# Threshold attention and Fourier mixing: the softmax sums closed by one reduce, and two small jobs moved from GpSimd to ScalarE

## The chip, the cores and the metric

The kernel runs on one core of a Trainium2 chip. The metric is the device time of one execution in microseconds (us); lower is better. Five engines work side by side, each through its own queue in program order: TensorE (PE; its weight loads are listed as PEld), VectorE (DVE), ScalarE (ACT), GpSimd (POOL), and SyncE (SP), which here issues nearly all DMAs.

## The reference

Attention with a threshold, followed by a Fourier mixing block with a two-layer network. B = 8 batches, 8 heads, 576 rows, head dimension 64, so a model width of 512; all in float32 (the two weight matrices arrive in float64 bits).

```python
scores = scale * np.matmul(q, k.transpose(0, 1, 3, 2))
thresh = np.max(scores, axis=-1, keepdims=True) - tau
scores = np.where(scores >= thresh, scores, -1000000000.0)
scores = scores - np.max(scores, axis=-1, keepdims=True)
attn = np.exp(scores)
attn = attn / (np.sum(attn, axis=-1, keepdims=True) + 1e-09)
x = np.matmul(attn, v)                      # then heads side by side: (B, S, 512)

mixed = np.real(np.fft.fft(np.fft.fft(x, axis=1), axis=2))
u = x + mixed
un = (u - np.mean(u)) / np.sqrt(var + 1e-06)   # mean and var over the last axis
out = u + np.maximum(un @ w_ch1, 0.0) @ w_ch2
```

## The kernel before

The order of all instructions is written out by hand; no planner moves them. The attention is cut into steps. A pair of heads has five steps (`t = i % NT`): in `t` 0 to 3, 128 query rows of both heads, and in `t` 4 the last 64 rows of both heads in one tile of 128 rows, so that such a step has one head column only (`nh` is 1). A batch has four pairs, so 20 steps.

Each step begins with `scores`, on TensorE (L427, L433), into PSUM. The softmax then takes these instructions: the row maximum, negated, on VectorE (L451); exp on ScalarE (L459), and right behind the first exp a small ScalarE instruction that makes the threshold `thr` (L463); then on VectorE the masking (L467), which multiplies the exps by the comparison with the threshold and adds up the row into `den` with an accumulator output. 1e-9 is added to each sum (L472, one element per row, after each head), and both are inverted (L481). The two masked tiles are turned by TensorE in the next step (`transposed_weights(i - 1)`, L578 to L600) and multiplied by v in `weighted_values` (L627).

The inverse sums are used in two ways. In the first two batches (steps 0 to 39) GpSimd copies them with repetition into `rec`, 128 columns (L493); TensorE transposes `rec` beside the last columns of the weights (L581), and the product with v is multiplied by it on VectorE (L636). From step 40 on the weights themselves are scaled, by ScalarE (L540).

q is multiplied by the scale in place before it is transposed: for the first pair and from the third batch on by ScalarE (L385), for the other pairs of the first two batches by GpSimd (L387), in step `t == 2`; VectorE transposes k and q in step `t == 3` (L398 to L401), and only then SyncE loads the next pair into the same tiles.

Three loops run over the steps. `step(i)` for batch 0 adds the conversion of the first weight matrix from float64 bits, in stages over VectorE (L293, L296, L308), ScalarE (L301, L304, L315) and GpSimd (L313, L316), with small TensorE fillers (L111) and the subtraction of column means (L373). `second_batch(i)` for steps 20 to 39 adds the conversion of the second weight matrix, the mixing of batch 0 (L750 to L796), and the first group of the network (`channels`: L877 on TensorE, evacuated alternately by ScalarE, L882, and VectorE, L884). Its filling work is given out by `fill`, from a budget that depends on counts alone and not on time. From step 40 on the third loop uses `softmax_first`, `softmax_second` and `softmax_third`; there the sums of a step get their 1e-9 in one instruction of up to two elements (L531) and are inverted (L534), and the network runs as two levels of a fast matrix product (L1163, L1306 on TensorE, with additions on VectorE and GpSimd).

In `step`, ScalarE's queue holds per step: exp, `thr`, exp, the last conversion stage of the chunk before (L315), the copies of the transposed weights of step i - 1 (L584, L598), and the first stages of the present chunk (L301, L304). In a step with `t == 4`, a copy of 64 weight columns (L497) stands right behind the softmax.

Of the kernel before, what the change touches and what calls it, by code (L numbers as in the profile page):

```python
# [9 lines left out]
FP32 = mybir.dt.float32  # L10
INT32 = mybir.dt.int32
UINT32 = mybir.dt.uint32
ALU = mybir.AluOpType
# [34 lines left out]
def kernel(  # L48
# [12 lines left out]
    nc = tc.nc  # L61
# [5 lines left out]
    NT = 5  # L67
# [305 lines left out]
        eng.tensor_tensor(out=w1[c][:, cols], in0=rows, in1=means[g][:, :], op=ALU.subtract)  # L373


    heads = {}
    steps = {}
    xs = {}
# [2 lines left out]
    def scale_q(n):  # L381

        raw = loaded[n][0]
        if n == 0 or late:
            nc.scalar.activation(out=raw[:, :], in_=raw[:, :], func=ACT.Copy, scale=q_scale[:, :])  # L385
        else:
            nc.gpsimd.tensor_scalar(  # L387
                out=raw[:, :], in0=raw[:, :], scalar1=q_scale[:, :], scalar2=None, op0=ALU.mult
            )

    def prep_pair(n):

# [46 lines left out]
    def softmax(i, between=None, meanwhile=None, behind=None):  # L439


        t = i % NT
        sc, nh = steps[i]
        neg = sb.tile([128, 2], FP32, tag="neg", bufs=3, name="neg")
        thr = sb.tile([128, 2], FP32, tag="thr", bufs=3, name="thr")
        den = sb.tile([128, 2], FP32, tag="den", bufs=3, name="den")


        e = sb.tile([128, 2 * S], FP32, tag="e", name="e")
        for j in range(nh):  # L450
            nc.vector.tensor_reduce(  # L451
                out=neg[:, j : j + 1], in_=sc[j][:, :, 0:HALF], axis=AXIS_XY, op=ALU.max,
                negate=True,
            )
        if meanwhile is not None:
            meanwhile()
        for j in range(nh):
            ej = e[:, S * j : S * (j + 1)].rearrange("p (c n) -> p c n", c=2)
            nc.scalar.activation(  # L459
                out=ej, in_=sc[j][:, :, 0:HALF], func=ACT.Exp, bias=neg[:, j : j + 1], scale=1.0  # L460
            )
            if j == 0:
                nc.scalar.activation(  # L463
                    out=thr[:, 0:nh], in_=neg[:, 0:nh], func=ACT.Identity,
                    bias=thr_off[:, :], scale=-1.0,
                )
            nc.vector.scalar_tensor_tensor(  # L467
                out=ej, in0=sc[j][:, :, 0:HALF], scalar=thr[:, j : j + 1], in1=ej,
                op0=ALU.is_ge, op1=ALU.mult, accum_out=den[:, j : j + 1],
            )  # L470

            nc.vector.tensor_scalar(  # L472
                out=den[:, j : j + 1], in0=den[:, j : j + 1], scalar1=1e-9, scalar2=None,
                op0=ALU.add,
            )
# [5 lines left out]
        nc.vector.reciprocal(den[:, 0:nh], den[:, 0:nh])  # L481
        rec = None
        if normalized(i // NT):
            nc.vector.tensor_scalar(
                out=e[:, 0:S], in0=e[:, 0:S], scalar1=den[:, 0:1], scalar2=None, op0=ALU.mult
            )
            if nh == 2:
                nc.scalar.activation(
                    out=e[:, S : 2 * S], in_=e[:, S : 2 * S], func=ACT.Copy, scale=den[:, 1:2]
                )  # L490
        else:
            rec = sb.tile([128, 2 * D], FP32, tag="rec", name="rec")
            nc.gpsimd.tensor_copy(  # L493
                rec[:, :].rearrange("p (j d) -> p j d", j=nh), _repeated(den[:, 0:nh], 2 * D // nh)
            )
        if t == 4:
            nc.scalar.copy(e[:, S : S + 64], e[:, 512:S])  # L497
        steps[i] = (e, rec)

    def softmax_first(i):  # L500
# [20 lines left out]

    def softmax_second(i):
        sc, nh, e, thr = steps[i]
        den = sb.tile([128, 2], FP32, tag="den", bufs=3, name="den")
        for j in range(nh):
            ej = e[:, S * j : S * (j + 1)].rearrange("p (c n) -> p c n", c=2)
            nc.vector.scalar_tensor_tensor(  # L527
                out=ej, in0=sc[j][:, :, 0:HALF], scalar=thr[:, j : j + 1], in1=ej,
                op0=ALU.is_ge, op1=ALU.mult, accum_out=den[:, j : j + 1],
            )  # L530
        nc.vector.tensor_scalar(  # L531
            out=den[:, 0:nh], in0=den[:, 0:nh], scalar1=1e-9, scalar2=None, op0=ALU.add
        )
        nc.vector.reciprocal(den[:, 0:nh], den[:, 0:nh])  # L534
        steps[i] = (nh, e, den)

    def softmax_third(i):
        nh, e, den = steps[i]
# [878 lines left out]
    def step(i):  # L1417

        n, t = divmod(i, NT)
        scores(i)  # L1420

        def stages(count):
            for _ in range(count if i - 1 in chunks else 0):
                next(chunks[i - 1], None)

        def next_stages():
            stages(2)

        def last_stage():
            stages(1)  # L1430
            chunks.pop(i - 1, None)

        if t == 1 and n > 0:
            softmax(i, lambda: weighted_values(n - 1, 1), next_stages, last_stage)
            load_v(n + 1)
        elif t == 3:
            softmax(i, lambda: weighted_values(n, 0), next_stages, last_stage)
        else:
            softmax(i, None, next_stages, last_stage)
        if t == 1 and n > 0:  # L1440
            pass
        elif later and later[0][0] <= i:
            later.pop(0)[1](i)
        else:
            busy(2 if i < NCHUNK else 1)
        if t == 2:
            scale_q(n + 1)
        if t == 3:
            prep_pair(n + 1)
        if t == 1:  # L1450
            prep_ends(n)
        if i in chunks:
            next(chunks[i])
        if i > 0:
            transposed_weights(i - 1)
        if i in chunks:
            next(chunks[i])
        while after and after[0][0] <= i:
            after.pop(0)[1]()
        if i > 0 and i + 3 < NCHUNK:  # L1460
            chunks[i + 3] = w1_chunk(i + 3)
        if t == 2 and n > 0:
            folds.append(fold_rows(n - 1))
        if folds and next(folds[0], True):
            folds.pop(0)

    folds = []
    later = []
# [91 lines left out]
    def second_batch(i):  # L1560

        nonlocal budget
        n, t = divmod(i, NT)
        first = i - per_batch
        if first != 1:
            scores(i)
        if first == 0:

            transposed_weights(i - 1)
        softmax(  # L1570
            i, None, lambda: (advance(first - 1), advance(first - 1)), lambda: advance(first - 1)
        )
        chunks.pop(first - 1, None)
        transfers(first)
        fold_more()
        if first == 0:
            weighted_values(n - 1, 1)
            scores(i + 1)
            column_means(LAST)
            copy_mean(LAST)  # L1580
            folds.append(fold_rows(n - 1))
            while folds:
                fold_more()
            load_v(n + 1)
            start_batch(0)
            mix(3)
            mix(3)
        elif first == 1:
            mix(3)
            transposed_weights(i - 1)  # L1590
            mix(2)
            mirrored(LAST)
            for c, eng in ((1, nc.vector), (3, nc.vector), (0, nc.gpsimd), (2, nc.gpsimd)):
                less_mean(eng, LAST, c)
            advance(first)
            advance(first)
        elif first == 2:
            mix(2)
            transposed_weights(i - 1)
            mix(2)  # L1600
            weighted_values(n, 0)
            advance(first)
            advance(first)
        else:
            fill()
            transposed_weights(i - 1)
            advance(first)
            advance(first)
# [135 lines left out]
```

## Time and profile before

The median of three runs is 1607.57 us (1606.21 to 1608.24). The profiled execution took 1605.7 us, of which the profile's span is 1603.8 us.

| part | value |
|---|---|
| span, instructions | 1603.8 us, 27061 |
| busy PE | 1537.4 us (96%) |
| busy VectorE | 1105.6 us (69%) |
| busy ScalarE | 908.4 us (57%) |
| busy GpSimd | 811.7 us (51%) |
| L472, add 1e-9, early | 72 instructions, mean 153 ns |
| L531, add 1e-9, late | 120 instructions: 96 of two elements, mean 352 ns; 24 of one, mean 154 ns |
| L493, rec, GpSimd | 40 instructions, mean 387 ns |
| L387, q scaled, GpSimd | 8 instructions, mean 1854 ns |
| L385, q scaled, ScalarE | 24 instructions, mean 771 ns |
| L497, copy of 64 columns, ScalarE | 8 instructions, mean 244 ns |

The page names an instruction group by its line, engine and operation, and by what it writes and reads (`out<-in`). In the order of time a row gives the start and the length in us; a bracket at its end says how long the engine was idle before and what released it. A busy TensorE isn't TensorE at its peak, because matmuls are pipelined and their ends are modelled.

### The profile page before, as it was taken

How to read it: one execution, taken by the hardware profiler on the slowest of the kernel's cores; microseconds unless marked ns; L12 is line 12 of the kernel's file. 1: busy time of each engine (PE TensorE's matmuls, PEld its weight loads, DVE VectorE, ACT ScalarE, POOL GpSimd, SP SyncE). 2: the span in 40 equal slices, each digit the busy share in tenths (PEclk: the TensorE clock that was granted, in tenths of full speed). 3: DMA queues.
4: the chain of work that ended last, by engine and by line, in shares of the span. 5: the costliest groups of instructions: out<-in, count | busy, mean ns of one | idle time of the engine just before them, and what ended most of it. 6: DMA issues, size and time to landing. Idle time of an engine off the chain costs nothing.

```text
span 1603.8 us, 27061 instructions
## 1 busy us (share of the span) xinstructions
PE 1537.4 (96%) x9770; PEld 1189.2 (74%) x9770; DVE 1105.6 (69%) x2165; ACT 908.4 (57%) x1873; POOL 811.7 (51%) x1014
## 2 busy tenths in 40 slices
PE   8999979999999999999999999999999999999997
PEld 4555445555787778877787878787887778879997
DVE  7997886845869566766577566856676656746547
ACT  5774665554655666656666666656665665223121
POOL 6784664034455552536254724455263625537646
PEclk9999999999999999999999999999999999999998
DMA  6423221555956264634564355626463534546655
GB/s 158 131 57 115 75 76 36 175 158 164 291 159 203 72 182 125 182 104 141 141 175 140 113 159 145 191 69 180 123 185 108 154 113 158 191 157 237 235 193 190
DMA packets 245499, 239.05 MB, mean 149 GB/s; under 512 B 196947, under 2 KB 214869, under 8 KB 225014
## 3 DMA queue, kind: packets, MB, share of 16 engines
q1 hardware_dynamic: 242854, 237.02, 49.1%
q8 instruction: 78, 1.28, 0.3%
q10 hardware_dynamic: 2512, 0.30, 0.2%
q14 instruction: 55, 0.45, 0.1%
HBM read 207.50 MB, written 29.62 MB: 148 GB/s over the span
## 4 chain that ended last, share of the span: by engine, by line
PE 76%; DVE 14%; ACT 4%; issue 2%; POOL 2%; DMA 1%; SPq 0%; DVEq 0%; ACTq 0%; POOLq 0%
PE ph L1163 24%; PE po L1306 17%; PE pv L627 8%; PE sc L427 7%; PE pw L596 6%; PE po L901 4%; PE ph L877 2%; PE py L750 2%; DVE e L467 2%; PE sc L433 1%; PE pa L767 1%; PE pe L578 1%; PE pa L771 1%; DVE neg L451 1%; ACT e L512 1%
## 5 line engine op out<-in xcount | busy, mean ns | idle before, releaser
L512 ACT ACTIVATE e<-sc,neg 128x576 f32<-128x576 f32 x216 | 158.6, 734 | 139.8 <-DVE neg L506 139.4
L506 DVE TENSOR_REDUCE neg<-sc 128x1 f32<-128x576 f32 x216 | 154.0, 749 | 112.0 <-PE sc L427 104.1
L1306 PE MATMUL po<-w,w_all 128*128 128x128 f32 x1792 | 229.1, 278 | 0.7 <-ACT ends L584 0.7
L1306 PEld LDWEIGHTS po<-w,w_all 128*128 128x128 f32 x1792 | 214.7, 193 | 10.2 <-issue 5.5
L1100 DVE TENSOR_TENSOR hs<-ph,hs 128x512 f32<-128x512 f32 (+1 forms) x128 | 105.1, 821 | 158.5 <-PE ph L1163 104.0
L1109 POOL TENSOR_TENSOR w<-hs 128x512 f32<-128x512 f32 x32 | 42.1, 1320 | 318.9 <-ACT hs L1105 245.1
L596 PE MATMUL pw<-ident,e 128*128 128x128 f32 x1152 | 172.1, 276 | 18.0 <-ACT x_first L634 9.1
L1163 PE MATMUL ph<-u_t,w 128*128 128x256 f32 x768 | 180.5, 381 | 0.5 <-DMA w<-f 0.4
L527 DVE SCALAR_TENSOR_TENSOR e<-sc,thr,e 128x576 f32<-128x576 f32 x216 | 168.1, 811 | 17.7 <-ACT thr L516 17.7
L427 PE MATMUL sc<-kT,qT 64*128 64x288 f32 x1024 | 170.3, 432 | 7.9 <-DVE e L467 7.9
L598 ACT COPY e_t<-pw 128x512 f32<-128x512 f32 x256 | 148.5, 594 | 45.8 <-PE pw L596 44.6
L540 ACT ACTIVATE e<-e,den 128x576 f32<-128x576 f32 x216 | 157.6, 775 | 16.6 <-DVE den L534 15.4
L596 PEld LDWEIGHTS pw<-ident,e 128*128 128x128 f32 x1152 | 136.3, 142 | 36.3 <-ACT x_first L634 10.1
L1163 PE MATMUL ph<-w_all,w 128*128 128x256 f32 x672 | 157.0, 382 | 2.9 <-DVE hs L1100 1.8
L1163 PEld LDWEIGHTS ph<-u_t,w 128*128 128x128 f32 x768 | 141.2, 190 | 23.4 <-issue 4.4
L1105 ACT ACTIVATE hs<-hs 128x512 f32<-128x512 f32 (+1 forms) x96 | 74.1, 772 | 122.0 <-DVE hs L1100 120.8
L1163 PEld LDWEIGHTS ph<-w_all,w 128*128 128x128 f32 x672 | 123.5, 190 | 25.6 <-issue 6.2
L427 PEld LDWEIGHTS sc<-kT,qT 64*128 64x128 f32 x1024 | 93.9, 186 | 62.9 <-issue 32.8
L1213 POOL TENSOR_TENSOR w_all<-w_all 128x128 f32<-128x128 f32 (+2 forms) x160 | 118.5, 758 | 29.9 <-DVE w_all L1326 22.4
L1306 PE MATMUL po<-w,hs 128*128 128x128 f32 x960 | 126.3, 279 | 0.0
L1306 PEld LDWEIGHTS po<-w,hs 128*128 128x128 f32 x960 | 116.2, 193 | 9.4 <-issue 7.2
L792 POOL TENSOR_TENSOR u_t<-x,tmp 128x289 f32<-128x289 f32 (+1 forms) x45 | 34.5, 766 | 104.8 <-DVE tmp L787 104.8
(221 smaller groups left out, 2985.1 us busy)
## 6 DMA issues: line engine op xcount, KB each, us to landing
w<-f SPq DMA_DIRECT2D x152, 1024.0 KB, 4.9
hs<-in_moe_w_ch_dram SPq DMA_DIRECT2D x23, 512.0 KB, 4.6
q_in<-in_q_dram SPq DMA_DIRECT2D x128, 72.0 KB, 3.9
out_dram<-u SPq DMA_DIRECT2D x36, 256.0 KB, 2.5
k_in<-in_k_dram SPq DMA_DIRECT2D x124, 72.0 KB, 3.0
v_in<-in_v_dram SPq DMA_DIRECT2D x64, 128.0 KB, 4.7
f<-w SPq DMA_DIRECT2D x14, 512.0 KB, 4.0
f<-w SPq DMA_DIRECT2D x7, 1024.0 KB, 4.4
```

Source lines behind the costliest of these rows:

```text
L427: nc.tensor.matmul(sc[j][:, c, 0:HALF], qT[hp, 128 * t : 128 * t + 128], kT[hp, k0 + HALF * c : k0 + HALF * (c + 1)], start=True, stop=True,)
L506: nc.vector.tensor_reduce(out=neg[:, j : j + 1], in_=sc[j][:, :, 0:HALF], axis=AXIS_XY, op=ALU.max, negate=True,)
L512: nc.scalar.activation(out=ej, in_=sc[j][:, :, 0:HALF], func=ACT.Exp, bias=neg[:, j : j + 1], scale=1.0)
L527: nc.vector.scalar_tensor_tensor(out=ej, in0=sc[j][:, :, 0:HALF], scalar=thr[:, j : j + 1], in1=ej, op0=ALU.is_ge, op1=ALU.mult, accum_out ...
L540: nc.scalar.activation(out=e[:, S * j : S * (j + 1)], in_=e[:, S * j : S * (j + 1)], func=ACT.Copy, scale=den[:, j : j + 1],)
L596: nc.tensor.transpose(pw[:, c, :], e[:, c0 : c0 + 128], ident[:, :])
L598: nc.scalar.copy(e_t[:, 4 * j : 4 * j + 4, qs], pw[:, :, :])
L627: nc.tensor.matmul(pv[64 * j : 64 * j + 64, 0:m], vt[:, 2 * c + j, :], e_t[:, 4 * j + c, 0:m] if c < 4 else ends[:, 0, 0:m], start=(c == 0 ...
L1100: nc.vector.tensor_tensor(out=to, in0=bank, in1=to if other is None else other, op=ALU.add)
L1163: nc.tensor.matmul(bank[:, 256 * q : 256 * q + 256].rearrange("p (two n) -> p two n", two=2), left[:, 256 * c + 128 * q : 256 * c + 128 * ...
L1213: return lambda: eng.tensor_tensor(out=to, in0=to, in1=other, op=ALU.add)
L1306: nc.tensor.matmul(to, lefts[m][j][:, s], right_[:, 128 * s : 128 * (s + 1)], start=(jn in (0, 4) or cut and jn > 4) and s == 0, stop=s == ...
```

## The change

Three things are changed.

The 1e-9 is no longer added by an instruction of its own. Three tiles `den_eps` of two columns per head are filled with 1e-9 once. The masking writes each row sum into the first column of its head, so that sum and 1e-9 lie side by side; a reduce over the last axis then gives sum plus 1e-9 for both heads at once, and the reciprocal follows. A helper, `inverse`, does this for all three loops. In the early softmax this also takes the instruction between the two heads' maskings away.

`rec` is written by ScalarE and no longer by GpSimd, by a new function `spread_inverse` that is called at the very end of each step of the first two batches. The copy of 64 columns of `t == 4` moves there too.

q is scaled by ScalarE in all pairs.

```diff
+    den_eps = [const.tile([128, 2, 2], FP32, name=f"den_eps{u}") for u in range(3)]
+    for den in den_eps:
+        nc.vector.memset(den[:, :, :], 1e-9)
+
+    def inverse(i, nh):
+        den = sb.tile([128, 2], FP32, tag="den", bufs=3, name="den")
+        nc.vector.tensor_reduce(
+            out=den[:, 0:nh], in_=den_eps[i % 3][:, 0:nh, :], axis=AXIS_X, op=ALU.add
+        )
+        nc.vector.reciprocal(den[:, 0:nh], den[:, 0:nh])
+        return den
...
     def scale_q(n):
 
         raw = loaded[n][0]
-        if n == 0 or late:
-            nc.scalar.activation(out=raw[:, :], in_=raw[:, :], func=ACT.Copy, scale=q_scale[:, :])
-        else:
-            nc.gpsimd.tensor_scalar(
-                out=raw[:, :], in0=raw[:, :], scalar1=q_scale[:, :], scalar2=None, op0=ALU.mult
-            )
+        nc.scalar.activation(out=raw[:, :], in_=raw[:, :], func=ACT.Copy, scale=q_scale[:, :])
...
             nc.vector.scalar_tensor_tensor(
                 out=ej, in0=sc[j][:, :, 0:HALF], scalar=thr[:, j : j + 1], in1=ej,
-                op0=ALU.is_ge, op1=ALU.mult, accum_out=den[:, j : j + 1],
-            )
-
-            nc.vector.tensor_scalar(
-                out=den[:, j : j + 1], in0=den[:, j : j + 1], scalar1=1e-9, scalar2=None,
-                op0=ALU.add,
+                op0=ALU.is_ge, op1=ALU.mult, accum_out=den_eps[i % 3][:, j, 0:1],
             )
...
-        nc.vector.reciprocal(den[:, 0:nh], den[:, 0:nh])
-        rec = None
+        den = inverse(i, nh)
...
+            steps[i] = (e, None)
         else:
-            rec = sb.tile([128, 2 * D], FP32, tag="rec", name="rec")
-            nc.gpsimd.tensor_copy(
-                rec[:, :].rearrange("p (j d) -> p j d", j=nh), _repeated(den[:, 0:nh], 2 * D // nh)
-            )
-        if t == 4:
+            steps[i] = (e, den[:, 0:nh])
+
+    def spread_inverse(i):
+        e, den = steps[i]
+        if i % NT == 4:
             nc.scalar.copy(e[:, S : S + 64], e[:, 512:S])
+        if den is None:
+            return
+        nh = den.shape[1]
+        rec = sb.tile([128, 2 * D], FP32, tag="rec", name="rec")
+        nc.scalar.copy(
+            rec[:, :].rearrange("p (j d) -> p j d", j=nh), _repeated(den, 2 * D // nh)
+        )
         steps[i] = (e, rec)
...
     def softmax_second(i):
...
-        nc.vector.tensor_scalar(
-            out=den[:, 0:nh], in0=den[:, 0:nh], scalar1=1e-9, scalar2=None, op0=ALU.add
-        )
-        nc.vector.reciprocal(den[:, 0:nh], den[:, 0:nh])
-        steps[i] = (nh, e, den)
+                op0=ALU.is_ge, op1=ALU.mult, accum_out=den_eps[i % 3][:, j, 0:1],
+            )
+        steps[i] = (nh, e, inverse(i, nh))
...
@@ -1463,6 +1464,7 @@   (end of step)
             folds.append(fold_rows(n - 1))
         if folds and next(folds[0], True):
             folds.pop(0)
+        spread_inverse(i)
...
@@ -1624,6 +1626,7 @@   (end of second_batch)
         if first < 3:
             budget += 3 * per_slot
+        spread_inverse(i)
```

More of the change, by code (lines that the diff above doesn't have):

```diff
@@ L445, in softmax @@
         thr = sb.tile([128, 2], FP32, tag="thr", bufs=3, name="thr")
-        den = sb.tile([128, 2], FP32, tag="den", bufs=3, name="den")
         e = sb.tile([128, 2 * S], FP32, tag="e", name="e")
@@ L523, in softmax_second @@
         sc, nh, e, thr = steps[i]
-        den = sb.tile([128, 2], FP32, tag="den", bufs=3, name="den")
         for j in range(nh):
@@ L528, in softmax_second @@
                 out=ej, in0=sc[j][:, :, 0:HALF], scalar=thr[:, j : j + 1], in1=ej,
-                op0=ALU.is_ge, op1=ALU.mult, accum_out=den[:, j : j + 1],
+                op0=ALU.is_ge, op1=ALU.mult, accum_out=den_eps[i % 3][:, j, 0:1],
             )
-        nc.vector.tensor_scalar(
-            out=den[:, 0:nh], in0=den[:, 0:nh], scalar1=1e-9, scalar2=None, op0=ALU.add
-        )
-        nc.vector.reciprocal(den[:, 0:nh], den[:, 0:nh])
-        steps[i] = (nh, e, den)
+        steps[i] = (nh, e, inverse(i, nh))
     def softmax_third(i):
```

## The prediction

> **What bounds the kernel now.** I read the chain of work that ended last, then the busy time by stretch, then the order of time on each engine at the lines that the change touches. The page's chain by engine:
>
> ```profile
> PE 76%; DVE 14%; ACT 4%; issue 2%; POOL 2%; DMA 1%; SPq 0%; DVEq 0%; ACTq 0%; POOLq 0%
> ```
>
> The stretches say where the part that is not TensorE lies (columns: stretch, length, then busy time of PE, PEld, DVE, ACT, POOL, the granted clock, DMA share, GB/s):
>
> ```profile
> 40.00:80.00 40.00, 37.53 (x195) 21.31 (x194) 38.38 (x84) 31.80 (x63) 30.79 (x37) 1.00 0.49 132
> 80.00:120.00 40.00, 36.52 (x184) 20.68 (x184) 37.20 (x81) 28.12 (x57) 32.60 (x37) 0.96 0.25 57
> 400.00:800.00 400.00, 390.94 (x2604) 318.50 (x2604) 279.27 (x542) 251.67 (x514) 191.81 (x241) 0.99 0.55 161
> ```
>
> Up to some 127 us (batch 0, 20 steps) VectorE is full, 37 to 38 of 40 us; TensorE's figure there contains its filler matmuls. From 290 us TensorE is full: 98%, and VectorE at 70% has air. Between 127 and 290 us (batch 1) the chain changes hands. So a microsecond of VectorE is worth most in batch 0 and almost nothing after 290 us.
>
> Inside a step of batch 0, in order of time (start, length, engine, line), first the early softmax, then a late one and its neighbours:
>
> ```profile
> 103.41 0.82 DVE L467 SCALAR_TENSOR_TENSOR e<-sc,thr,e 128x576 f32<-128x576 f32 x1 [0.16 <-ACT thr L463]
> 104.15 0.08 DVE L467 DVE_READ_ACCUMULATOR e<-sc,thr,e 128x1 f32 x1
> 104.27 0.15 DVE L472 TENSOR_SCALAR den<-den 128x1 f32<-128x1 f32 x1
> 104.34 0.81 DVE L467 SCALAR_TENSOR_TENSOR e<-sc,thr,e 128x576 f32<-128x576 f32 x1
> ...
> 105.19 0.15 DVE L472 TENSOR_SCALAR den<-den 128x1 f32<-128x1 f32 x1
> 105.38 0.17 DVE L481 RECIPROCAL den<-den 128x2 f32<-128x2 f32 x1
> ...
> 858.14 0.80 DVE L527 SCALAR_TENSOR_TENSOR e<-sc,thr,e 128x576 f32<-128x576 f32 x1
> 858.88 0.81 DVE L527 SCALAR_TENSOR_TENSOR e<-sc,thr,e 128x576 f32<-128x576 f32 x1
> 859.61 1.27 POOL L1121 TENSOR_TENSOR hs<-hs,w 128x512 f32<-128x512 f32 x1
> 859.73 1.17 DVE L531 TENSOR_SCALAR den<-den 128x2 f32<-128x2 f32 x1
> 860.93 0.17 DVE L534 RECIPROCAL den<-den 128x2 f32<-128x2 f32 x1
> 861.01 0.47 DVE L863 SCALAR_TENSOR_TENSOR u<-w_all,rstd,u 128x256 f32<-128x256 f32 x1
> ```
>
> With the addition of 1e-9 between the heads the second masking starts 0.93 us after the first (104.34 - 103.41); without it, late, 0.74 us. And the late addition, on two elements, took 1.17 us, ending with GpSimd's instruction.
>
> [...] the one-element addition (L472) takes 153 to 155 ns always, the two-element one (L531) has a mean of 352 and a most of 1417 ns. No small reduce is in the trace. [...]
>
> **The change part by part.** Price of the new reduce: L506 reduces 576 elements in 748 ns; [...] against the addition's 153. I take them as equal, an issue distance of 0.19 us (105.38 - 105.19). Bounds: 0.05 less, or 0.10 more if two rows of two cost extra.
>
> *Early additions.* Of 72, 32 go without successor (the first head's in two-head steps) and 40 become reduces. Each of the 32 is worth 0.93 - 0.74 = 0.19 us of VectorE.
>
> *Inverse sums (rec).* 40 GpSimd copies, mean 387 ns, become ScalarE copies. Price: the exp's neighbour L497 copies 64 columns in 244 ns; [...] It stands last in the step. Queued behind it: the next step's exp, thr, hence VectorE's masking; and TensorE waits for rec with its transpose (L581). In batch 0 the queue has no gap just there:
>
> ```profile
> 82.22 0.70 ACT L304 ACTIVATE hs<-hs,shift 128x512 int32<-128x512 int32 x1
> 82.83 0.72 ACT L459 ACTIVATE e<-sc,neg 128x576 f32<-128x576 f32 x1
> ```
>
> I went through the 20 hand-overs from step to step, comparing thr's end with the end of VectorE's instruction before the masking. Seven (steps 1, 8, 12, 15 to 18 to their next) have idle ScalarE or wait for scores: full gain, 7 x 0.19 = 1.33 us. Six are tight, VectorE later than ScalarE by only 0.07 to 0.17: they keep 0.06 to 0.14 each, 0.70 together. Three are set by ScalarE (3, 10, 13): -0.19 + 0.20, nothing. In the four one-head steps (4, 9, 14, 19) nothing is saved, and the copy L497 (244 ns, 0.15 of queue) moves to the step's end too, 0.35 with rec; minus the slack of 0.15 in two of them: 0.22 + 0.21 + 0.36 + 0.35 = 1.14 lost. At 17.88 us TensorE waits 1.92 us for rec, but VectorE only follows at 22.97: 0.3 gained. [...] (0.51 against 0.41 us): 0.1 in about five steps that VectorE sets, 0.5. Batch 0: -1.33 - 0.70 - 0.30 - 0.50 + 1.14 = -1.7 us.
>
> *q scaled (8 copies).* GpSimd 1.85 us each become ScalarE 0.76 (L385), 0.64 of queue. No DMA moves: q's load follows VectorE's transpose. In batch 0 (steps 2, 7, 12, 17) ScalarE waits there 1.33, 0.69, 0.60+0.26 and 1.7 us: covered; without that cover 0.64 each. In batch 1 it stands just before rec; at step 22 the 0.84 us delay falls into VectorE's 1.47 us wait for TensorE (168.79), save 0.1; at 27, 32, 37 ScalarE waits over 3 us.
>
> *Batch 1.* Mix start, step 20: +0.2 (exp behind rec). GpSimd's u_t chain at 156.58 loses a rec: -0.3. Step 22: +0.1. Step 24: copies behind L882, so TensorE's transposes at 175.28 go only at about 177.3; much of it is under VectorE's and ScalarE's chain: +0.4. Steps 25, 27 and 38, masking and reduce: -0.19, -0.3, -0.19; step 28: -0.24. Step 26: ScalarE delivers at 193.9 what GpSimd did at 193.8: 0. Step 29: +0.37; step 31: +0.2; step 34: +0.05. Step 36 is the dearest:
>
> ```profile
> 270.78 0.27 PE L581 MATMUL pe<-ident,rec 128*128 128x128 f32 x1
> ...
> 271.43 0.20 ACT L855 ACTIVATE warm<-eps 128x1 f32<-128x1 f32 x1
> ```
>
> Here rec falls behind two table loads that end with L855, so the transpose comes at about 271.9 in the middle of a TensorE chain: +0.95. The sum is +1.0.
>
> *Late steps.* 120 additions become reduces: [...] nearly all under TensorE. What TensorE does lose there is four stalls like this one (the addition above, 8 us of full VectorE, exp, the copy that frees a bank):
>
> ```profile
> 869.33 0.44 PE L596 MATMUL pw<-ident,e 128*128 128x128 f32 x2 [2.19 <-ACT x_first L634]
> ```
>
> But L863, next on VectorE, [...] 860.88 instead of 861.01. I take 4 x 0.13 = 0.5 us; the bounds are 0 and 4 x 1.0.
>
> Sum: -1.7 + 1.0 - 0.5 = -1.2 us. The profiled execution took 1605.7 (span 1603.8 and 1.9 around it), so 1604.5; the runs' median of 1607.57 lies 1.9 higher, so 1606.4 on its scale.
>
> **Rivals.** [...] If L863 doesn't wait, the four stalls give 4.0 instead of 0.5: 1606.4 - 3.5 = 1602.9. For it: L863's median is 0.48 and many of its neighbours are GpSimd's; against: the tiny two-input L690 took 1.12 us beside GpSimd.
> *ScalarE's queue comes to set the end (slower).* The spread, last in the queue, may be late for TensorE. If rec takes its full 0.30 us because it waits on VectorE's semaphore (20 tight steps, +2.0), and TensorE's waits at steps 24, 29, 31 and 36 count in full (2.05 + 0.45 + 0.70 + 0.95 = 4.15 against my 1.97, +2.2), and the scaling at step 22 isn't covered (+0.6): 1606.4 + 4.8 = 1611.2. It decides once ScalarE ends a step later than TensorE ends the next scores, about 1.2 us. For it: ScalarE was only 0.07 to 0.17 us ahead in six steps. Against: after 227 us ScalarE waits 1 to 4 us per step for its maxima.
> *The reduce is dearer (no change).* 0.10 us x about 25 on the chain: 1608.9. The kernel would still be within the bound. That it isn't executed as written is unlikely; all 160 steps call it.
>
> **Chances and range.** 0.2% is 3.2 us, about what a measurement of this kernel can tell from none. The forecast and the dearer reduce, both within it: 0.48. [...]: 0.27. ScalarE sets the end: 0.25. The likeliest case alone spans 1604.6 to 1609.0; to leave out no more than 2 in 10 the range reaches both rivals, 1601.9 to 1611.4.
>
> **What would show it.** Right: maskings 0.74 us apart in the first 40 steps; reduces of about 0.15 us without a long tail; rec on ScalarE near 0.3 us; a transpose of rec waiting near 271 us; four late stalls still near 2 us, with L863 at 1.2 to 1.3 us in its place; start of the late steps about 0.7 us earlier than 288. Wrong: TensorE waits on ScalarE's rec of over 4 us in all, or the late stalls down to 1.2 us.

## Result: no measurable difference, from two effects of several microseconds

| | before | after |
|---|---|---|
| median | 1607.54 us | 1606.47 us |
| ratio, 95% interval | | 0.9994 (0.9986 to 1.0002) |
| profiled execution, its span | 1605.7, 1603.8 us | 1604.92, 1603.1 us |
| busy VectorE, ScalarE, GpSimd | 1105.6, 908.4, 811.7 us | 1090.0, 919.8, 787.2 us |

The forecast was 1606.4 us. That it came out so near is partly luck, as the experiments show. The moves cost much more than the terms given to them, the reduce gains at least what its terms said but in other places, and the two cancel. Besides, the runs of the changed kernel had a slightly higher clock than those of before (0.9878 against 0.9866), which by the line fitted below is worth about 1 us.

The profile after: the chain by engine, the line that answers to the one of before.

```profile
PE 74%; DVE 15%; ACT 4%; issue 2%; DMA 2%; POOL 2%; SPq 1%; ACTq 0%; DVEq 0%; POOLq 0%
```

The stretches after (stretch, length, then busy time of PE, PEld, DVE, ACT, POOL, the granted clock, DMA share, GB/s):

```profile
40.00:80.00 40.00, 37.20 (x195) 21.00 (x193) 38.11 (x77) 32.88 (x72) 26.39 (x29) 1.00 0.46 127
80.00:120.00 40.00, 35.64 (x175) 20.65 (x176) 36.84 (x75) 29.92 (x65) 31.15 (x35) 0.91 0.25 57
400.00:800.00 400.00, 391.42 (x2599) 319.82 (x2598) 272.89 (x541) 250.84 (x513) 192.59 (x241) 0.99 0.53 160
```

In the first stretch VectorE runs seven instructions fewer (77 for 84), and yet it is as full as before: 38.11 us against 38.38. What the instructions left free, it spends in longer ones. That is the first sign that the saving did not reach the end of the batch. The second stretch has a granted clock of 0.91 (0.96 before), to which the section on the hardware comes back.

The new instructions, each by its line (count, then shortest, median and longest in ns):

```profile
L382 DVE TENSOR_REDUCE den<-den_eps x160: 154/157/158, 15.0 to 1351.9; 128x2 f32<-128x4 f32 x128, 128x1 f32<-128x2 f32 x32
L501 ACT COPY rec<-den x40: 279/286/323, 17.0 to 290.6; 128x128 f32<-128x128 f32 x40
L396 ACT ACTIVATE q_in<-q_in,q_scale x32: 758/762/812, 7.0 to 1297.3; 128x576 f32<-128x576 f32 x32
```

All three prices hold: 157 ns for the reduce (taken as equal to the addition's 153), 286 for rec (near 0.3 us), 762 for the scaling (760). The longest of 160 reduces is 158 ns, beside a GpSimd that is busy half of the time (787.2 of 1603.1 us): none shows a wait like that of the two-element addition, whose longest took 1417 ns. That rec takes 0.20 us of ScalarE's queue was the author's estimate; in this trace the next instruction, where it waits for nothing, starts 186 to 200 ns after rec.

Where the difference of 0.7 us between the two spans comes from can be read at VectorE's reciprocals, of which there is one in each step. Step 20's is at 133.22 us (before 132.89), step 40's at 294.67 (292.30). So the changed kernel enters the late steps 2.4 us later, not 0.7 earlier as predicted, and gains 3.1 us afterwards. Part of each figure goes with the clock. At 104.4 us the changed kernel has a fall of the clock to half that is twice as long (6.8 us) as the one of before at 106.7 (3.4 us); e9 (below), which has the same code there and a single fall, is 0.8 us less behind from step 15 to 17. And 2.65 of the 3.1 us are gained behind the last softmax, where before has such a double fall at 1383 us and the changed kernel none.

The late stall after the change, the same place as the one at 859.73 us before, in the order of time:

```profile
862.65 1.27 POOL L1122 TENSOR_TENSOR hs<-hs,w 128x512 f32<-128x512 f32 x1
862.78 0.16 DVE L382 TENSOR_REDUCE den<-den_eps 128x2 f32<-128x4 f32 x1
862.97 0.17 DVE L385 RECIPROCAL den<-den 128x2 f32<-128x2 f32 x1
863.05 1.15 DVE L864 SCALAR_TENSOR_TENSOR u<-w_all,rstd,u 128x256 f32<-128x256 f32 x1
...
869.57 0.30 PE L579 MATMUL pe<-ident,e 128*128 128x128 f32 x1 [0.25 <-DVE w_all L1327]
872.06 0.79 PE L597 MATMUL pw<-ident,e 128*128 128x128 f32 x4 [2.19 <-ACT x_first L635]
```

The wait for GpSimd has moved from the addition to L864 (L863 before), 0.47 to 1.15 us, which ends 0.28 us behind GpSimd's L1122, and the stall of 2.19 us is still there: both as predicted. The gain sits in the line between: TensorE's wait for `w_all` fell to 0.25 us, from 0.56 in the row of before:

```profile
866.84 0.30 PE L578 MATMUL pe<-ident,e 128*128 128x128 f32 x1 [0.56 <-DVE w_all L1326]
```

The same 0.31 us is gained at four places (at the first, 0.90 became 0.59), 1.25 us in all; the sum had 0.13 each.

### The profile page after: what moved, and what is told of

Read it like the earlier page. It is cut to its first block, busy times and chain, and to the rows that moved or that the text cites. A ratio compares the mean times of both kernels' runs of the same rounds, so it can differ in the third digit from the quotient of the medians.

```text
span 1603.1 us, 26985 instructions
## 1 busy us (share of the span) xinstructions
PE 1534.1 (96%) x9770; PEld 1187.3 (74%) x9770; DVE 1090.0 (68%) x2136; ACT 919.8 (57%) x1921; POOL 787.2 (49%) x966
## 4 chain that ended last, share of the span: by engine, by line
PE 74%; DVE 15%; ACT 4%; issue 2%; DMA 2%; POOL 2%; SPq 1%; ACTq 0%; DVEq 0%; POOLq 0%
PE ph L1164 24%; PE po L1307 17%; PE pv L628 9%; PE sc L434 7%; PE pw L597 6%; PE po L902 4%; PE ph L878 2%; PE py L751 2%; DVE e L471 2%; PE sc L440 1%; PE pa L768 1%; DVE neg L455 1%; PE pa L772 1%; PE pe L579 1%; ACT e L518 1%
```

## The experiments

One kernel's times scatter by up to 9 us, mostly with the mean granted clock of the run, which is the share of TensorE's full clock that it was given. The time lost to the clock is (1 - clock) x span, 13 to 27 us. One straight line through all runs, with a constant for each kernel, gives 0.50 us of time for each microsecond lost in this way. The last column of the table compares each kernel with before at the same loss. It is a second reading of the same runs, not a second measurement, and the clock is known to three digits only (0.8 us). The intervals are those of the fit alone: the four groups of runs of before, on four chips, differ among themselves by up to 0.6 us at the same loss. And if a kernel raises its own clock, this column takes that gain away from it.

| kernel | median us | ratio to before, 95% | mean clock | at equal clock, us |
|---|---|---|---|---|
| before | 1606.16 to 1607.12 | | 0.9866 | 0 |
| after | 1606.47 | 0.9994 (0.9986 to 1.0002) | 0.9878 | +0.2 ± 0.6 |
| e1 reduce only | 1601.20 | 0.9965 (0.9952 to 0.9978) | 0.9890 | -3.6 ± 1.0 |
| e2 moves only | 1613.69 | 1.0038 (1.0026 to 1.0050) | 0.9864 | +6.1 ± 0.9 |
| e3 after, unread GpSimd copy | 1602.19 | 0.9976 (0.9967 to 0.9985) | 0.9886 | -2.0 ± 0.6 |
| e4 after, q on GpSimd | 1604.92 | 0.9985 (0.9979 to 0.9991) | 0.9880 | -0.8 ± 0.5 |
| e5 early reduce only | 1604.17 | 0.9986 (0.9978 to 0.9994) | 0.9880 | -1.4 ± 0.6 |
| e6 late reduce only | 1602.26 | 0.9978 (0.9969 to 0.9987) | 0.9882 | -2.5 ± 0.6 |
| e7 reduce twice, early | 1604.70 | 0.9987 (0.9979 to 0.9995) | 0.9869 | -2.4 ± 0.5 |
| e8 reduce, q on ScalarE | 1600.81 | 0.9970 (0.9958 to 0.9981) | 0.9884 | -4.1 ± 1.0 |
| e9 after, step 36 spread early | 1604.74 | 0.9985 (0.9977 to 0.9994) | 0.9888 | -0.4 ± 0.6 |
| e10 e3 and e9 | 1603.31 | 0.9979 (0.9971 to 0.9988) | 0.9890 | -1.6 ± 0.6 |
| e11 after, step 36 on GpSimd | 1603.11 | 0.9982 (0.9974 to 0.9991) | 0.9887 | -1.2 ± 0.5 |
| e12 after, first batch on GpSimd | 1602.15 | 0.9982 (0.9972 to 0.9991) | 0.9890 | -1.5 ± 0.6 |

The traces give a reading that is free of the clock. Between step 3 and step 14 no fall of the clock lies in any of the traces used here (e6 and e8 have one and are left out). Where two kernels have the same code, such distances repeat closely: from step 3 to 36 the changed kernel and e11 keep theirs within 0.07 us. How much later a kernel's reciprocal of step 14 comes, compared with before, than its reciprocal of step 3:

| inverse sums of the first batch on | kernels | later by, us |
|---|---|---|
| GpSimd | e1, e5, e7, e12 | -0.19, -0.18, +0.03, -0.89 (of which -0.51 is q's scaling) |
| ScalarE | after, e2, e4, e9, e11 | +0.77, +1.15, +0.57, +0.72, +0.72 |
| ScalarE, and an unread copy on GpSimd | e3, e10 | -0.41, -0.36 |

### Which part gives, which takes (e1, e2)

e1 is the changed kernel with q's scaling, the copy of the inverse sums and the place of the 64-column copy as before; e2 has these three as in the change and keeps the additions. Each has five runs.

```diff
 # e1, in softmax, right behind den = inverse(i, nh)
-            steps[i] = (e, den[:, 0:nh])
+            rec = sb.tile([128, 2 * D], FP32, tag="rec", name="rec")
+            nc.gpsimd.tensor_copy(
+                rec[:, :].rearrange("p (j d) -> p j d", j=nh), _repeated(den[:, 0:nh], 2 * D // nh)
+            )
 # e2, in softmax and in softmax_second
-                op0=ALU.is_ge, op1=ALU.mult, accum_out=den_eps[i % 3][:, j, 0:1],
+                op0=ALU.is_ge, op1=ALU.mult, accum_out=den[:, j : j + 1],
 # ... and the additions of 1e-9 as before
```

> Only the reduce of the change, in all 160 steps; inverse sums and q scaling stay on GpSimd. Read at VectorE's reciprocal of step 20 (132.89 us before, 133.22 after) and of step 40 (292.30 before, 294.67 after), at the duration of the 512-wide shift L296 in the first batch, and at the time. Theory [...] (the moved copies let two long GpSimd instructions follow each other, and L296 waits for the second): L296 as before (0.51 in steps 8, 11 and 13), step 20 at 130.9 to 131.7, step 40 at 290 to 291.3, and about 1.3 us more gained in the late steps: 1604 to 1605. Rival, that the reduce itself is the dearer part (0.10 us more than the addition): step 20 at 133 or later, and no gain.

> Only the moves: inverse sums and q scaling on ScalarE, the additions of 1e-9 as before. [...] the moves cost what the reduce saves: step 20's reciprocal at 134.3 to 135.5, step 40's at 295 to 297, the late steps as before, 1609 to 1612. If my recorded sum were right (moves +1.1 in the first batch, about +1.5 in the second): step 20 at 134.0, step 40 at 295. If the moves cost nothing: 132.9 and 292.3.

The reduce alone is faster by 0.35%, the moves alone are slower by 0.38%. By the ratios the two cancel, as was measured for the change. At equal clock they sum to +2.5 us, with about 1 us of doubt in each, where the change has +0.2 ± 0.6: beside the reduce the moves cost 3.8 ± 1.1 us (the changed kernel against e1), less than the 6.1 that they cost alone. Where this difference lies wasn't found. In e2 step 20's reciprocal is at 135.16 us and step 40's at 298.56: 2.3 and 6.3 us later than before; the second, and the time, are worse than either theory had said. In e1 they are at 132.34 and 291.98. Both are 0.6 to 0.7 us later than the first theory's forecast, but L296 is at 0.51 us in steps 8, 11 and 13, as that theory wants, and the time is 3 us better than its forecast. That the reduce is the dearer part is refuted.

### Where the reduce gains (e5, e6, e7)

e5 has the reduce in `softmax` only, e6 in `softmax_second` only. e7 is e1 with one more instruction in each of the first 40 steps:

```diff
+        spare = sb.tile([128, 2], FP32, tag="spare", bufs=3, name="spare")
+        nc.vector.tensor_reduce(
+            out=spare[:, 0:nh], in_=den_eps[i % 3][:, 0:nh, :], axis=AXIS_X, op=ALU.add
+        )
         den = inverse(i, nh)
```

> The reduce only in the first 40 steps; everything else, the late additions too, as before. The reduce alone (all 160 steps) gave 1601.2 against 1607.1, of which its trace shows only 0.3 us at step 40. Theory: [...] (VectorE's L293 waits for GpSimd's L316 to end in most steps), so the early part gives almost nothing: step 20's reciprocal at 132.3 to 133.0, step 40's at 291.5 to 292.7, time 1606 to 1607.3, mean granted clock 0.986 as before. Rival (my recorded sum: a full microsecond and a half from the first batch): step 20 at 131.3 or earlier, time 1604 to 1605.5.

> The reduce only from step 40 on; the first 40 steps as before. Theory: nearly all of the gain lies here, in two parts: the three waits of TensorE for w_all (0.56 us each, before the long stalls) go, some 1.3 to 2 us; and TensorE's clock falls to half less often behind these stalls, another 2 to 4 us: step 40 within 0.5 us of 292.3, time 1602 to 1604, mean clock 0.988 to 0.990. Rival (my recorded sum: 0.5 us late, no effect on the clock): 1606.5, clock 0.986.

> The reduce alone, with a second reduce of the same shape before it in each of the first 40 steps, into a tile that nobody reads: 0.19 us more of VectorE in each step, 3.8 us in the first batch. Theory of GpSimd's cover: [...] step 20's reciprocal at 132.3 to 133.3 (the reduce alone 132.34), time 1601 to 1602.5. Rival (VectorE full, each instruction counts): step 20 at 135 to 136.2, time 1604 to 1606.

Both halves count: e5 0.14% and e6 0.22% faster, which add up to e1. e5's time, 1604.17 us, lies in the range of the rival and not in that of my theory; its step 20, at 131.70 us, lies between the two. In its trace 1.2 us are gained at step 20, of which 0.5 was there by step 3; from step 3 to 20 both e5 and e1 gain 0.73 us. e6's trace keeps step 40 at 292.92 and shows the four shorter waits of TensorE (5.2 us for `w_all` before, 4.0 in e6), so 1.2 us; the rest of its 2.5 isn't accounted for. A stall of 0.77 us behind ScalarE's `x` at 416 us is gone in e6, but it is gone in e2 and e5 too, which have the code of before there, so it isn't the reduce's. Its clock was 0.9882, higher than before, but so was that of e5, which leaves the late steps alone. That the shorter waits raise the clock is therefore not shown.

e7 tests the cover in the first batch. Its second reduce costs VectorE less than I had written: it depends on nothing and follows the first by 0.08 us (73.11 and 73.19), not 0.19, so 17 steps from 3 to 20 add 1.4 us. Of these 0.2 us arrived (-0.54 against -0.73 for e1). The rest came out of L293, which waits for GpSimd. The line of L293 in the first batch of before (shortest, median, longest ns):

```profile
L293 DVE TENSOR_SCALAR w<-hs x16: 385/958/1411, 15.1 to 105.5; 128x512 int32<-128x512 int32 x16
```

The same line of e1, the reduce alone:

```profile
L293 DVE TENSOR_SCALAR w<-hs x16: 384/1140/1531, 14.8 to 105.3; 128x512 int32<-128x512 int32 x16
```

And of e7, with the reduce made twice:

```profile
L293 DVE TENSOR_SCALAR w<-hs x16: 385/1068/1482, 14.4 to 103.9; 128x512 int32<-128x512 int32 x16
```

A free L293 takes 385 ns (at 35.50 us of before, where GpSimd is idle). Before, eleven of the 16 end 0.28 us behind an instruction of GpSimd, seven of them behind L316. The median is 958 before; it grows by 182 ns in e1, just what a saved addition is worth (0.19), and gives 72 back in e7 (0.08). VectorE is full in the first batch, but some of its busy time is waiting for GpSimd, and a shorter softmax only waits longer. The time of the whole kernel, 1604.70 us, lies in the rival's range all the same: e7 is slower than e1, at equal clock by 1.2 ± 1.0 us. In the traces 0.2 of this lies in the first batch and 0.95 between step 20 and 40, where the second reduce is made too and both have falls of the clock. So the cover is shown for the first batch alone.

### Why the moved copy costs: GpSimd's long instructions close up (e3, e12)

Step 10 to 11 of before, VectorE and GpSimd in the order of time (start, length, engine, line):

```profile
74.55 1.29 POOL L316 TENSOR_TENSOR w<-w,hs 128x512 f32<-128x512 f32 x1
...
75.01 1.11 DVE L293 TENSOR_SCALAR w<-hs 128x512 int32<-128x512 int32 x1
75.78 0.49 POOL L493 COPY rec<-den 128x128 f32<-128x128 f32 x1
...
76.04 0.51 DVE L296 TENSOR_SCALAR hs<-hs 128x512 int32<-128x512 int32 x1
...
76.23 1.46 POOL L373 TENSOR_TENSOR w<-w,mean 128x512 f32<-128x512 f32 x1
```

The same of the changed kernel:

```profile
72.32 0.81 DVE L471 SCALAR_TENSOR_TENSOR e<-sc,thr,e 128x576 f32<-128x576 f32 x1
...
73.06 1.29 POOL L316 TENSOR_TENSOR w<-w,hs 128x512 f32<-128x512 f32 x1
73.17 0.16 DVE L382 TENSOR_REDUCE den<-den_eps 128x2 f32<-128x4 f32 x1
...
73.45 1.18 DVE L293 TENSOR_SCALAR w<-hs 128x512 int32<-128x512 int32 x1
74.30 1.46 POOL L373 TENSOR_TENSOR w<-w,mean 128x512 f32<-128x512 f32 x1
...
74.55 1.49 DVE L296 TENSOR_SCALAR hs<-hs 128x512 int32<-128x512 int32 x1
```

L293 ends 0.28 us behind L316 in both. Before, GpSimd then made its small copy, and L296 (76.04) was issued ahead of the long L373 (76.23). After, GpSimd has no copy to make, L373 (74.30) is ahead of L296 (74.55), and L296 lasts until 0.28 us after L373's end (75.76): 1.49 instead of 0.51 us. The two instructions are the same in both traces; the order in which they start isn't. The same happens to L296 in step 8 (1.03) and step 13 (1.01), there behind L679, and to L308 at 101.87 us (1.85 instead of 0.68).

e3 gives GpSimd its copy back without any use for it; e12 really goes back to GpSimd in the first 20 steps.

```diff
 # e3, in softmax
         den = inverse(i, nh)
+        spare = sb.tile([128, 2 * D], FP32, tag="spare", name="spare")
+        nc.gpsimd.tensor_copy(
+            spare[:, :].rearrange("p (j d) -> p j d", j=nh), _repeated(den[:, 0:nh], 2 * D // nh)
+        )
 # e12, in softmax
-        else:
+        elif i < 20:
+            ...                     # rec on GpSimd, as in e1
```

> The changed kernel, and GpSimd also makes the copy of the inverse sums that it made before, into a tile that nobody reads. Theory [...]: this additional work makes the first batch faster, since it parts GpSimd's long instructions again: L296 back to about 0.51 us in steps 8, 11 and 13 (1.03, 1.49, 1.01 after), step 20's reciprocal at 131.2 to 132.5 against 133.22. Theory of ScalarE's queue (the copies on ScalarE delay exp): step 20 at 133.2 or later, since ScalarE's order is the same and GpSimd has more to do. Time: 1605 to 1606 by the first, 1606.5 to 1608 by the second.

> The changed kernel, with the inverse sums of the first batch (20 steps) copied by GpSimd as before, those of the second by ScalarE. Theory: in the first batch the moved copy costs because GpSimd's long instructions close up (2.0 to 2.5 us), in the second because of ScalarE's queue (2.0): L296 at 0.51 us in steps 8, 11 and 13; from step 3 to step 20 VectorE gains 0.5 to 0.8 us on before, as with the reduce alone (the changed kernel loses 1.64); from step 20 to 40 it loses 1.8 to 2.4. Time at the same clock about 2 us under the changed kernel's. Rival (the copies of the first batch cost nothing by themselves, other clock falls do): no difference to the changed kernel from step 3 to 14.

e3 does 40 copies more than the changed kernel and is faster than before by 0.24%, at equal clock 2.2 ± 0.8 us faster than the changed kernel. Step 20 is at 130.34 us, earlier still than expected; no fall of the clock lies before it. Its trace at the same place:

```profile
73.34 1.11 DVE L293 TENSOR_SCALAR w<-hs 128x512 int32<-128x512 int32 x1
...
74.11 0.49 POOL L482 COPY spare<-den 128x128 f32<-128x128 f32 x1
...
74.37 0.51 DVE L296 TENSOR_SCALAR hs<-hs 128x512 int32<-128x512 int32 x1
...
74.56 1.46 POOL L373 TENSOR_TENSOR w<-w,mean 128x512 f32<-128x512 f32 x1
```

ScalarE's order in e3 is that of the changed kernel, so its queue isn't the cause in the first batch; the gap in GpSimd's is. e12 says the same from the other side: L296 at 0.51 in the three steps, 0.89 us gained from step 3 to 14. From step 3 to 20 it gains 1.37 us, more than the 0.5 to 0.8 expected; 0.51 of it is q's scaling, as e8 shows in the next section. From step 20 to 40 it loses 2.05 us, as expected and like the changed kernel (2.04).

### The scaling of q (e4, e8)

e4 is the changed kernel with `scale_q` of before, e8 is e1 with `scale_q` of the change.

```diff
 # e8 against e1; e4 against the changed kernel is the reverse
-        if n == 0 or late:
-            nc.scalar.activation(out=raw[:, :], in_=raw[:, :], func=ACT.Copy, scale=q_scale[:, :])
-        else:
-            nc.gpsimd.tensor_scalar(
-                out=raw[:, :], in0=raw[:, :], scalar1=q_scale[:, :], scalar2=None, op0=ALU.mult
-            )
+        nc.scalar.activation(out=raw[:, :], in_=raw[:, :], func=ACT.Copy, scale=q_scale[:, :])
```

> The changed kernel with the scaling of q back on GpSimd (8 times 1.85 us). By my recorded sum the scaling costs ScalarE nothing in the first batch and saves 0.1 us in the second: step 20 and 40 within 0.5 us of the changed kernel's 133.22 and 294.67. If the scaling on ScalarE is what delays (TensorE waits 1.43 us for the ends at 85.64, 0.40 before): step 20 some 0.6 to 2 us earlier. If GpSimd's scaling holds VectorE up [...] (L308 1.20 us at 24.77 and 89.98 before, 0.68 after): 0.5 to 1 us later.

> The reduce and the scaling of q on ScalarE; the inverse sums stay on GpSimd. By my recorded sum the scaling costs nothing in the first batch and 0.1 us less in the second: 1601 to 1601.5, like the reduce alone. If the scaling on ScalarE delays the ends for which TensorE waits (0.6 us each in the first four, as at 85.64 us of the changed kernel): 1602 to 1603.5, step 20 at 133 to 134. If it frees VectorE [...] (L308 1.20 us twice): 1600 to 1601.

e8 equals e1 (ratios 0.9970 and 0.9965, intervals that cover each other): with the inverse sums on GpSimd the move of the scaling costs nothing in time. In the traces it even gains in one place: from step 12 to 13 e8 and e12 are both 0.51 us faster than e1, since L308 takes 0.68 us there and not 1.20 (e1 at 89.97 us, before at 89.98).

e4 is 1.0 ± 0.7 us faster than the changed kernel at equal clock, but its trace doesn't show that q's scaling on ScalarE costs this. e4's step 20 is 0.6 us later than the changed kernel's and its step 40 0.8 us earlier. The distance stays at 0.6 up to step 30 and turns at step 31, where the product with v runs into a fall of the clock in the changed kernel (half clock from 223.90 to 227.31 us), and in e4 doesn't. The row of the changed kernel, then that of e4:

```profile
224.09 3.95 PE L628 MATMUL pv<-e_t,v_rev 128*64 128x320 f32 x16 [2.82 <-ACT e_t L601]
...
225.01 2.38 PE L633 MATMUL pv<-e_t,v_rev 128*64 128x320 f32 x16 [0.79 <-ACT e_t L606]
```

One wait does differ (TensorE for the ends, 1.43 us at 85.64 in the changed kernel, 0.77 in e4, 0.40 before), but it brings e4 no more than 0.2 us. Why e4 is faster in time stays open.

### The table loads of step 36 (e9, e11, e10)

The second batch loses 2.0 us in the changed kernel, 1.14 of it from step 36 to 38. The trace there:

```profile
269.96 0.17 DVE L385 RECIPROCAL den<-den 128x2 f32<-128x2 f32 x1
270.01 1.28 ACT L853 ACT_TABLE_LOAD   x1
...
271.62 1.28 ACT L856 ACT_TABLE_LOAD   x1
...
273.02 0.28 ACT L501 COPY rec<-den 128x128 f32<-128x128 f32 x1
...
273.36 0.33 PE L582 MATMUL pe<-ident,rec 128*128 128x128 f32 x1 [0.93 <-ACT rec L501]
```

The inverse is there at 270.13; its copy comes 2.9 us later, and TensorE waits 0.93 us. e9 moves the copy ahead of the loads, e11 gives this one copy to GpSimd, e10 is e9 with e3's unread copy.

```diff
 # e9, in second_batch, right behind softmax(...)
+        if first == 16:
+            spread_inverse(i)
 # ... and at the end of the step only where first != 16
 # e11: as e12, with i == 36 in the place of i < 20
```

> The changed kernel with one line moved: in step 36 the copy of the inverse sums stands right behind the softmax on ScalarE, ahead of the two table loads (L853, L856), instead of at the step's end. Theory (rec behind the table loads holds TensorE for 0.93 us at 273.36, and this stays to the end of the batch): from the reciprocal of step 36 to that of step 38 the changed kernel loses 1.14 us against before; here 0.0 to 0.2. Rival (the loss comes from VectorE's or GpSimd's work around it): 0.8 or more stays lost. Time 0.5 to 1.2 us under the changed kernel's, about 1605 to 1606.

> The changed kernel, with the inverse sums of step 36 alone copied by GpSimd, as before the change. Moving this copy ahead of the table loads left the loss where it was (1.08 us from step 36 to 38), since the loads then waited behind VectorE's reciprocal. Theory: the loss belongs to ScalarE's queue of this one step, whatever the order in it; off that queue it goes: 0.0 to 0.2 us lost from step 36 to step 38 (1.14 in the changed kernel), time 0.5 to 1.3 us under the changed kernel's at the same clock. Rival (it comes from the copies of the steps before or from the clock): 0.8 or more stays.

> Both repairs: GpSimd's unread copy, which parts its long instructions, and step 36's spread ahead of the table loads. If GpSimd's spacing and the table loads are what the moved copies cost, this is as fast as the reduce alone, within 1 us of it: 1601 to 1602.5, with L296 at 0.51 us in steps 8, 11 and 13 and 0.0 to 0.2 us lost from step 36 to 38. If a third cost of the moves is left (ScalarE's queue in the other steps): 1603 to 1604.5.

e9 failed: TensorE no longer waits for rec, and still 1.08 us are lost from step 36 to 38. Its trace shows why:

```profile
270.05 0.30 ACT L501 COPY rec<-den 128x128 f32<-128x128 f32 x1 [1.45 <-DVE den L385]
...
271.61 1.28 ACT L853 ACT_TABLE_LOAD   x1
...
273.22 1.28 ACT L856 ACT_TABLE_LOAD   x1
273.23 0.18 DVE L857 RECIPROCAL rstd<-rstd 128x4 f32<-128x4 f32 x1 [3.27 <-ACT rstd L853]
...
273.92 0.75 DVE L455 TENSOR_REDUCE neg<-sc 128x1 f32<-128x576 f32 x1
```

ScalarE now sits 1.45 us in front of the copy until VectorE has the inverse, the table loads come 1.6 us later, and VectorE waits 3.27 us for what follows them, with the next step's maxima behind. The wait has only changed its place. In e11 the loss from step 36 to 38 is 0.00 us, and the kernel is 1.4 ± 0.8 us faster than the changed one at equal clock. So the loss belongs to ScalarE's queue of this step, in whatever order.

e10 (1603.31) doesn't reach the reduce alone, as its second expectation says; but step 36's loss is still in it (1.14), so its time doesn't show a third cost of the moves. The traces do. From step 20 to 26, with no fall of the clock in any of them, the changed kernel, e3, e4, e10, e11 and e12 lose 0.53 to 0.79 us against before; e1, e5, e6 and e8, whose inverse sums are copied by GpSimd, lose 0.04 to 0.33. (e2 and e9 have a fall there, e7 a second reduce.) It is spread over the steps and wasn't taken apart further. Behind step 26 falls of the clock shift such distances by up to 1.8 us: e10 has the code of e3 up to step 36, and yet gains 0.37 us from step 20 to 36 where e3 loses 1.11.

## Why the prediction was right, and where its steps were wrong

The time and the verdict were right; the steps, one by one:

- **Prices.** Reduce, rec and scaling were within 5% of what the traces show. The maskings are 0.74 us apart in two-head steps (71.58 and 72.32), as forecast.
- **Early additions: wrong in size.** "Each of the 32 is worth 0.93 - 0.74 = 0.19 us of VectorE", seven hand-overs "full gain", 2.0 us in all. e1 and e5 gain 0.73 us from step 3 to 20. I compared VectorE with ScalarE at each hand-over and left out GpSimd: L293 (median 958 ns, 385 free) mostly lasts until GpSimd's instruction is over and swallows the saving.
- **L296 shorter without GpSimd's copies, -0.5 us: wrong in sign.** At five places L296 did fall, from 0.51 us to between 0.41 and 0.45. At three others the free GpSimd starts its next instruction earlier (L373 in step 11, L679 in steps 8 and 13), and L296 lasts until that one is over, about 1 us longer in step 11 alone (e1, e3, e12).
- **Four one-head steps, +1.14 us: not there.** From 4 to 5, 9 to 10 and 19 to 20 the changed kernel loses nothing (-0.15, -0.09, -0.17). From 14 to 15 it loses 0.59, but by L308 (1.85 us) behind two GpSimd instructions that closed up.
- **Start, -0.3: open.** The wait for rec at 20 us is gone, and at step 3 the changed kernel is 1.31 us ahead of before. But e6, which has the old code there, is 0.89 ahead, and e9 and e11, which have the new, are 0.71 and 1.52 ahead: the start scatters by more than the term.
- **q scaled, nothing in the first batch and +0.1 in the second: no cost is shown in the traces.** Beside GpSimd's inverse sums it gains 0.51 us at step 13 (e8), by a shorter L308 (0.68 us for 1.20) that the sum hadn't looked at. Beside ScalarE's, e4 and the changed kernel lose the same from step 20 to 29 (0.78 and 0.76). That e4 is 1.0 ± 0.7 us faster in time is open. (My expectation for e4 read the +0.1 as a gain.)
- **Second batch, +1.0: half.** The changed kernel loses 2.04 us from step 20 to 40. Step 36 was put at +0.95 and measured 1.14, with the transpose waiting 0.93 us for rec behind the two loads, as described; e11 confirms it. The small terms of the other steps were to cancel with the reduce's gain, and came to +0.9.
- **Late, -0.5: right in kind, too small.** L864 takes over the wait, the 2.19 us stalls stay; 4 x 0.31 instead of 4 x 0.13. I had let L863 start where GpSimd's instruction ends (860.88 instead of 861.01), but what counts is the end of L864: it comes 0.28 us behind GpSimd's instruction, where that of L863, with the reciprocal still to do, came 0.60 behind it.
- **Signs named as wrong.** TensorE's waits for ScalarE's rec were to stay under 4 us. They came to 5.5, so this sign did appear. It was badly chosen: before, TensorE waited 4.6 us for GpSimd's rec.

In the second rival, the 1.97 for four steps is 1.92; it contains step 34's 0.05. This changes nothing.

So the rival in which ScalarE sets the end was partly true. The terms of the moves sum to about +2.3 us (1.14 - 0.30 - 0.50 in the first batch, 1.97 in the second), and at equal clock they cost +3.8 ± 1.1 beside the reduce, +6.1 ± 0.9 alone. ScalarE's queue is shown for 1.14 us of it (step 36), GpSimd's closed-up instructions for about 1 us (step 3 to 14, the changed kernel against e1). The terms of the reduce sum to about -3.5 us (2.03, 0.92 and 0.5), and it brought -3.6 ± 1.0 at equal clock, -5.9 by the medians: too much was expected of the first batch (2.0 for 0.73 from step 3 to 20), too little of the late steps (0.5; e6 has 2.5 ± 0.6). The forecast of -1.2 us met the measured -1.1 because these errors cancelled, and because the changed kernel's runs had the higher clock; at equal clock the change is worth +0.2 ± 0.6.

The best version is the reduce without the move of the inverse sums: e1 0.9965 and e8 0.9970 of the time before, 5 to 6 us faster than both kernels by the medians, about 4 at equal clock, from five runs each.

## What to carry to other kernels

An engine's busy time can hold waits for another engine, as that of L293 did here (385 ns free, 958 at the median). Before pricing a saved instruction, look whether the next one on that engine already waits for the other engine: in e1 the saving of 0.19 us lengthened L293 by 182 ns. A small instruction on the other engine can be what lets a long one through; taking GpSimd's copy away changed the order of issue, and L296 then took 1.49 us for 0.51, behind an L373 of 1.46. In a queue that holds a long job, a copy can be wrong at either end of it: in step 36 it cost 1.14 us behind the table loads, 1.08 ahead of them, and nothing in GpSimd's queue.

## What the runs showed of the hardware

The granted clock of TensorE fell to half for pieces of 3.4 us (0.50 from 521.00 to 524.00 us of the changed kernel), and which stalls have one behind them differs from trace to trace. Two late stalls of the changed kernel, each in the stretch up to its end and the one behind it (columns as above):

```profile
866.00:872.00 6.00, 3.62 (x31) 2.81 (x25) 6.00 (x11) 1.82 (x5) 2.07 (x1) 1.00 0.51 180
872.00:876.00 4.00, 3.94 (x20) 3.13 (x21) 3.89 (x11) 3.16 (x9) 0.00 (x0) 0.57 0.16 59
...
1213.00:1218.00 5.00, 3.08 (x25) 2.67 (x23) 5.00 (x10) 1.37 (x3) 1.99 (x1) 1.00 0.55 184
1218.00:1222.00 4.00, 3.50 (x28) 2.96 (x29) 3.92 (x10) 3.85 (x10) 0.09 (x1) 1.00 0.25 98
```

Both stalls last 2.19 us, from 869.87 to 872.06 and from 1216.31 to 1218.50. Behind the first the clock is 0.57, behind the second it stays at 1.00. In one trace the falls lie a whole number of 3.413 us apart (before: from 21.3 to 106.7 and to 519.7 us, 25 and 146 pieces), and a single fall lasts 3.413 us itself. Counted in steps of 3.413 us from the falls of the changed kernel, a step runs from 869.02 to 872.44. It holds the whole first stall, TensorE is busy in it for 0.98 us, and the fall follows at its end. The second stall is shared by two steps, with an edge at 1217.18; TensorE is busy for 2.31 and 2.10 us in them, and no fall follows. So the same stall can fill most of one step, or be shared by two. In the two traces, before and after, all 15 such steps at full clock in which TensorE was busy for 1.50 us or less were followed by half clock, and of those with 1.53 us or more only one was (2.09 us, from 103.25 us of before). What the clock goes by isn't shown beyond this count.

At half clock a piece costs up to 1.7 us (an estimate: half of 3.413), and it can cost nothing: e10 lost 1.5 us against e3 by a double fall at 103.4 us, and e1 nothing that lasts against e12 by a single one at 106.3. After step 40 the profiled execution of before has six pieces, that of the changed kernel five, the last 9.0 and 7.1 us aside, where both run at half clock; with the 1.25 us of shorter waits this can explain up to 2.95 of the 3.1 us gained there. Traces of kernels that differ by a microsecond or two must be compared between two such falls, or the falls counted.

Further: an independent reduce of four elements follows another by 0.08 us (e7), a reciprocal that needs its result by 0.18 to 0.19.
